# Balanced routing on one core: the leftover search counts with the experts on the partitions and the thresholds in columns, and VectorE takes the digit with a 32x32 turn

## The chip, the cores and the metric

The kernel runs on one core of one Trainium2 chip. The metric is device time in microseconds (us) for one launch. Three runs of the kernel before gave 488.05 us as the median, with 486.91 and 488.65 us as the ends. A profiled execution took 487.56 us; the span between its first and its last instruction is 485.7 us.

## The reference, cut to what matters

Two blocks follow each other. The first is a gated linear attention (4 batches, 8 heads, 768 steps, head width 48). Its output is read as 3072 tokens of width 384. The second is a mixture of 8 experts with a hard balance: every expert takes exactly 384 tokens.

```
logits = x @ w_gate                       # 3072 x 8
order = np.argsort(-logits.flatten())
for idx in order:                         # best pair of token and expert first
    tok, e = idx // E, idx % E
    if assigned[tok] >= 0 or counts[e] >= cap: continue
    assigned[tok] = e; counts[e] += 1
for e in range(E):
    h = np.maximum(x[assigned == e] @ w1[e], 0.0)
    out[assigned == e] = h @ w2[e]
```

The loop over all pairs is serial. The kernel does it in rounds: every token that is still free votes for its best open expert, and a search finds the logit above which all votes can be granted because the fullest expert just reaches 384.

## The kernel before, in words

**Stages.** Attention runs to about 169 us of the span. Then one full search over all 3072 tokens (24 blocks of 128) closes the first expert, and all tokens that this search places get their slots. The tokens that it doesn't place, at most 768 (`NL` = 6 blocks of 128), are the leftovers; their rows of logits are fetched by six indirect DMAs into `lg` (lines 678 to 682). Rounds 1 to 7 of the leftover search (the loop at line 712) assign them, one round per expert that closes. The list of places is completed after that (lines 739 to 755), the rows of the third block of each expert can be fetched, and the remaining matmuls run.

**The expert matmuls as filler.** Two blocks of the experts 0 to 4 are already known before the leftover search, and their work is cut into pieces which wait in a queue, `pe_work`: a piece T turns one block of rows (three transposes, line 484), a piece H is one product of the up projection (line 495; 24 per expert), and a piece O is one product of the down projection (line 506; 16 per expert). One H or O piece is two MATMUL instructions in the trace, since the operands are 32 bit wide. All of this part stands under a manual schedule, so each engine executes its instructions in the order in which the program writes them.

**The planner that sets this order.** Two clocks in us, `pe` and `dve`, run along while the program is written. `V(n, cost)` (line 458) moves `dve` forward by the planned cost of VectorE instructions. `PE(cost)` (line 461) stands ahead of each group of small matmuls that depends on VectorE: it takes pieces from the queue until `pe` reaches `dve` + 0.1, then adds the group's own cost to `pe`, and sets `dve` to at least `pe` + 0.22. A piece costs 0.65 (T), 0.44 (H) or 0.65 (O) by this clock. It is arithmetic on constants; no run changes it.

**One digit of the search before** (`search`, line 550, called at line 718 with `n` = 6). The logits are scaled to whole numbers below 2^20, and the threshold is found in 4 digits of 5 bits. For each digit, VectorE writes `above`, 6 x 31 flags for each partition: is this token at or above threshold 1 to 31. TensorE counts with six matmuls (line 564), the flags as the weights (31 columns) and the one-hot choices of the expert (8 columns) as the moving operand; a seventh (line 567) adds what each expert holds already. The counts stand with thresholds on 31 partitions and experts in 8 columns. VectorE takes the largest over the experts (`most`, line 570) and compares with 384 (`filled`, line 571). A matmul with the constant weights `units[d]` (line 574) sums the flags over the partitions and writes the new `base` to all 128 partitions, from which `above` of the next digit subtracts.

**Around the digits.** After four digits, `sure` (line 720) marks the placed tokens, `more` and `now` (lines 726, 727) count them per expert, one matmul with `ones16` (line 731) sums over the partitions, and `pen`, `held`, `gone` and `lg` (lines 732 to 736) close full experts and placed tokens for the next round. At the head of the next round, `ov` and `ch` (lines 715, 716) are the best open logit of each token and its one-hot expert.

Of the kernel before, what the change touches and what calls it, by code (L numbers as in the profile page):

```python
# [12 lines left out]
FP16 = mybir.dt.float16  # L13
I32 = mybir.dt.int32
ALU = mybir.AluOpType
# [5 lines left out]
GONE = -1.0e9  # L21
# [3 lines left out]
def kernel(  # L25
# [11 lines left out]
    nc = tc.nc  # L37
# [3 lines left out]
    E = moe_w_gate.shape[1]  # L41
# [7 lines left out]
    NT = N // 128  # L49
    CAP = N // E  # L50
# [239 lines left out]
    DIGITS, BITS = 4, 5  # L290
    TH = (1 << BITS) - 1
    RANGE = float(1 << (DIGITS * BITS))
    NL = 6
    NQ = NL + TE * E
    NA = 5
    KC = E + 1

    def tt(out_, a, b, op):
        nc.vector.tensor_tensor(out=out_, in0=a, in1=b, op=op)  # L299

    def ts(out_, a, s1, op0, s2=None, op1=None):
        kw = {} if op1 is None else {"op1": op1}
        nc.vector.tensor_scalar(out=out_, in0=a, scalar1=s1, scalar2=s2, op0=op0, **kw)

    def stt(out_, a, s, b, op0, op1):
        nc.vector.scalar_tensor_tensor(out=out_, in0=a, scalar=s, in1=b, op0=op0, op1=op1)

    def reduce(out_, in_, op):
        nc.vector.tensor_reduce(out=out_, in_=in_, axis=AX_X, op=op)

    def rt(shape, name, dtype=FP32, bufs=2):
        return route.tile([128] + shape, dtype, name=name, tag=name, bufs=bufs)

    def mid_of(t, n):
        return t.unsqueeze(1).to_broadcast((128, n) + tuple(t.shape[1:]))

    def last_of(t, n):
        return t.unsqueeze(len(t.shape)).to_broadcast(tuple(t.shape) + (n,))
# [5 lines left out]
    ones16, after16 = const([128, 128], FP16, "ones16"), const([128, 128], FP16, "after16")  # L324
# [16 lines left out]
    def ramp(n, name, step, base):  # L341
        t = const([128, n], FP32, name)
        ts(t[:], linef[:, 0:n], float(step), ALU.mult, float(base), ALU.add)
        return t

    first = ramp(E, "first", -1, E)
    code_e = ramp(E, "code_e", -TE, NL + TE * (E - 1))
    steps, units = [], []
# [95 lines left out]
    def fast():  # L444
# [4 lines left out]
        def bank(name, tag):  # L449
            return psum.tile([128, 512], FP32, name=name, tag=tag, bufs=BUFS[tag])  # L450
# [7 lines left out]
        def V(n=1, cost=0.21):  # L458
            clock["dve"] += n * cost

        def PE(cost):
            while pe_work and clock["pe"] < clock["dve"] + 0.1:
                piece()
            clock["pe"] = max(clock["pe"], clock["dve"] + 0.1) + cost
            clock["dve"] = max(clock["dve"], clock["pe"] + 0.22)
# [84 lines left out]
        def search(over, choice, n, held):  # L550

            base = bank("base", "b")
            for d in range(DIGITS):
                above = rt([n, TH], f"above{n}", FP16)
                a, s = last_of(over, TH), mid_of(steps[d][:], n)
                if d == 0:
                    tt(above[:], a, s, ALU.is_ge)
                else:
                    stt(above[:], a, base[:, 0:1], s, ALU.subtract, ALU.is_ge)
                V(cost=0.15 + n * TH / 700)  # L560
                r = bank("cnt", "r")
                PE(0.03 * n + 0.1)
                for c in range(n):
                    nc.tensor.matmul(out=r[0:TH, 0:E], lhsT=above[:, c, :], rhs=choice[:, c, :],  # L564
                                     start=(c == 0), stop=(c == n - 1 and held is None))
                if held is not None:
                    nc.tensor.matmul(out=r[0:TH, 0:E], lhsT=ones16[:, 0:TH], rhs=held[:],
                                     start=False, stop=True)
                most, filled = rt([1], "most"), rt([1], "filled", FP16)
                reduce(most[0:TH], r[0:TH, 0:E], ALU.max)  # L570
                ts(filled[0:TH], most[0:TH], CAP - 0.5, ALU.is_ge)
                V(2)
                PE(0.06)
                nc.tensor.matmul(out=base[:, 0:1], lhsT=units[d][0:TH, :], rhs=filled[0:TH],
                                 start=(d == 0), stop=(d == DIGITS - 1), skip_group_check=True)
            return base

        def positions(kind, nk, n, code, notfirst_, held):

            incl = rt([nk, n], f"incl{n}", FP16)  # L580
            P = bank("P", "r")
            w = nk * n
            Pv = P[:, 0:w].rearrange("p (k c) -> p k c", c=n)
            PE(0.1)
            nc.tensor.matmul(out=Pv, lhsT=after16[:], rhs=kind[:], start=True, stop=False)
            nc.vector.tensor_tensor_scan(incl[:].rearrange("p k c -> p (k c)"), notfirst_,
                                         kind[:].rearrange("p k c -> p (k c)"), 0.0,
                                         op0=ALU.mult, op1=ALU.add)
            V(cost=0.1 + w / 350)
            PE(0.2)  # L590
            nc.tensor.matmul(out=Pv, lhsT=ones16[:], rhs=incl[:], start=False, stop=held is None)
            if held is not None:
                nc.tensor.matmul(out=Pv, lhsT=ones16[:], rhs=last_of(held, n), start=False,
                                 stop=True)
            sums = P[:, 256:256 + nk]
            total = rt([nk], f"total{n}", FP16)
            nc.vector.tensor_copy(out=total[:], in_=incl[:, :, n - 1])
            own, pos = rt([nk, n], f"own{n}"), rt([n], f"pos{n}")
            tt(own[:], Pv, kind[:], ALU.mult)
            reduce(pos[:], own[:].rearrange("p k c -> p c k"), ALU.max)  # L600
            q, line, blk = rt([n], f"q{n}"), rt([n], f"line{n}", FP16), rt([n], f"blk{n}", FP16)
            ts(q[:], pos[:], 0.5 - 64.0, ALU.add, 1.0 / 128.0, ALU.mult)
            ts(q[:], q[:], 12582912.0, ALU.add, -12582912.0, ALU.add)
            stt(line[:], q[:], -128.0, pos[:], ALU.mult, ALU.add)
            tt(blk[:], q[:], code, ALU.add)
            V(9)
            return total, line, blk
# [36 lines left out]
        with tc.manual_schedule(engines=engines):  # L644
            idle = rt([3 * 128], "idle", FP16, 1)
            nc.gpsimd.memset(idle[:], 1.0)
            base = search(over0[:], choice0, NT, None)
# [5 lines left out]
            total, line, blk = positions(kind, KC, NT, code[:],  # L653
                                         notfirst[:].rearrange("p k c -> p (k c)"), None)
# [18 lines left out]
            for e in range(1, NA):  # L673
                for i in range(2):
                    p = place_of(e, i)
# [19 lines left out]
            nc.vector.tensor_copy(out=val_l[:], in_=found[:, 0:NL])  # L695
            m = bank("m", "r")
            nc.tensor.matmul(out=m[:, 0:KC], lhsT=ones16[:], rhs=total[:], start=True, stop=True)
            few = rt([E], "few", FP32, 1)
            nc.vector.memset(few[:], 0.0)
            ts(few[:, 0:NA], m[:, 1:1 + NA], 2 * 128 - 0.5, ALU.is_lt)  # L700
# [4 lines left out]
            ts(pen[:], m[:, 1:KC], CAP - 0.5, ALU.is_ge, GONE, ALU.mult)  # L705
            held, got = rt([E], "held", FP16), rt([NL, E], "got", FP32, 1)
            stt(held[:], pen[:], 0.0, total[:, 1:KC], ALU.is_ge, ALU.mult)
            nc.vector.memset(got[:], 0.0)
            clock["dve"] = 15.0
            ts(lg[:], lg[:], low_scale[:, 0:1], ALU.add, low_scale[:, 1:2], ALU.mult)  # L710
            tt(lg[:], lg[:], last_of(gone[:], E), ALU.add)
            for rnd in range(1, E):
                tt(lg[:], lg[:], mid_of(pen[:], NL), ALU.add)
                ov, ch = rt([NL], "ov"), rt([NL, E], "ch", FP16)
                reduce(ov[:], lg[:], ALU.max)
                tt(ch[:], lg[:], last_of(ov[:], E), ALU.is_equal)
                V(3, 0.23)
                base = search(ov[:], ch, NL, held)
                sure, gone = rt([NL, E], "sure"), rt([NL], "gone")
                stt(sure[:], last_of(ov[:], E), base[:, 0:1], ch[:], ALU.is_ge, ALU.mult)  # L720
                tt(got[:], got[:], sure[:], ALU.add)
                V(2)
                if rnd == E - 1:
                    break
                more, now = rt([E], "more"), rt([E], "now", FP16)
                reduce(more[:], sure[:].rearrange("p c e -> p e c"), ALU.add)
                tt(now[:], held[:], more[:], ALU.add)
                V(2)
                PE(0.05)
                m2 = bank("m2", "r")  # L730
                nc.tensor.matmul(out=m2[:, 0:E], lhsT=ones16[:], rhs=now[:], start=True, stop=True)
                ts(gone[:], ov[:], base[:, 0:1], ALU.is_ge, GONE, ALU.mult)
                pen, held = rt([E], "pen"), rt([E], "held", FP16)
                ts(pen[:], m2[:, 0:E], CAP - 0.5, ALU.is_ge, GONE, ALU.mult)
                stt(held[:], pen[:], 0.0, now[:], ALU.is_ge, ALU.mult)
                tt(lg[:], lg[:], last_of(gone[:], E), ALU.add)
                V(4)

# [17 lines left out]
            for e in range(E):  # L756
                for i in range(2 if e < NA else 0, TE):
# [6 lines left out]
                             stop=False)  # L764
# [613 lines left out]
```

## Time and profile before

| what | value |
|---|---|
| median of three runs | 488.05 us (486.91 to 488.65) |
| the profiled execution's own time | 487.56 us |
| its span | 485.7 us |
| TensorE (PE) busy, share of the span | 454.8 us, 94% |
| VectorE (DVE) busy | 157.2 us, 32% |
| leftover search, first count to last base | 205.9 to 302.3 us of the span |
| mean granted clock of TensorE | 0.971 |

Times in the profile are us from the start of the span. PE is TensorE's matmuls, PEld its weight loads, DVE VectorE, ACT ScalarE, POOL GpSimd. In a row of the timeline stand the start, the length, the engine, the line of the kernel, the operation, what is written and read with sizes, how many instructions of this kind were merged, and in brackets how long the engine stood idle just before and what ended that. Lengths of matmuls include a tail that overlaps the next one, so the distance between starts says what one costs.

### The profile page before, as it was taken

Reading aid. Unit: us, or ns where it says so; the run is one execution under the profiler, and the core shown is the slowest. Engines: PE = TensorE matmul, PEld = TensorE weight load, DVE = VectorE, ACT = ScalarE, POOL = GpSimd, SP = SyncE. Lnnn points to the kernel's source line nnn. Section 1 sums busy time; section 2 is a strip of 40 time slices with the busy share of each in tenths; the row PEclk is TensorE's granted clock in tenths of the full one; section 3 lists DMA queues with packets and bytes.
Section 4 is the critical chain, followed back from the end, with each engine's and each line's share of the span. In section 5 each row is a group of like instructions: output and inputs, shape, how many; then the busy total and the mean of one; then the engine's idle time right before and its main releaser. Section 6 shows DMA issues by size and latency. Waiting matters only on the chain.

```text
span 485.7 us, 11676 instructions
## 1 busy us (share of the span) xinstructions
PE 454.8 (94%) x4996; PEld 323.1 (67%) x4996; DVE 157.2 (32%) x507; ACT 138.1 (28%) x366; POOL 105.2 (22%) x157
## 2 busy tenths in 40 slices
PE   2999999999999859999999999899999999999991
PEld 1778888887888635857566665768877656556550
DVE  7466655665667754123233332300000000000000
ACT  3455554555433100212121211213322312212200
POOL 3134333343223004710000101320003301301010
PEclk9999999999999857999999999999999999999996
DMA  9997999799931187960000000215993200200000
GB/s 152 188 166 164 190 198 202 158 194 263 245 141 52 55 305 267 312 225 17 18 17 1 32 1 16 68 51 198 301 319 95 66 0 34 66 16 34 0 34 20
DMA packets 118541, 59.28 MB, mean 122 GB/s; under 512 B 101840, under 2 KB 113104, under 8 KB 118480
## 3 DMA queue, kind: packets, MB, share of 16 engines
q1 hardware_dynamic: 111760, 44.06, 37.2%
q0 software_dynamic: 3264, 9.56, 6.5%
q10 hardware_dynamic: 3456, 4.82, 2.8%
q8 instruction: 41, 0.67, 0.6%
q14 instruction: 20, 0.16, 0.1%
HBM read 48.89 MB, written 9.54 MB: 120 GB/s over the span
## 4 chain that ended last, share of the span: by engine, by line
PE 73%; issue 15%; POOL 4%; DVE 4%; DMA 2%; ACT 0%; POOLq 0%; DVEq 0%
PE O L506 20%; PE H L495 19%; PE Y L225 5%; PE T L171 4%; PE A L208 4%; PE L L139 4%; PE L L143 3%; PE Y L235 2%; PE dS L190 2%; PE X L249 2%; PE cnt L564 2%; PE X L260 2%; DMA lg<-xd,at_l 2%; PE Xe L484 1%; POOL out_dram L512 1%
## 5 line engine op out<-in xcount | busy, mean ns | idle before, releaser
L495 PE MATMUL H<-xeT,w 128*128 128x256 f32 (+2 forms) x624 | 135.2, 369 | 2.0 <-DVE beyond L783 1.4
L506 PE MATMUL O<-w,hT 128*128 128x384 f32 x384 | 136.6, 494 | 0.0
L495 PEld LDWEIGHTS H<-xeT,w 128*128 128x128 f32 x624 | 97.7, 191 | 28.9 <-issue 1.6
L506 PEld LDWEIGHTS O<-w,hT 128*128 128x128 f32 x384 | 68.8, 190 | 37.0 <-issue 0.4
L512 POOL DMA_INDIRECT out_dram<-o,tok x24 | 23.5, 978 | 222.6 <-ACT o L511 218.4
L499 ACT ACTIVATE hT<-H 128x256 f32<-128x256 f32 (+2 forms) x104 | 38.2, 367 | 98.2 <-PE H L495 96.9
L213 DVE COPY_PREDICATED am<-mask,A 128x512 f32<-128x512 int32 x48 | 32.5, 732 | 30.8 <-PE A L208 30.8
L511 ACT COPY o<-O 128x384 f32<-128x384 f32 x24 | 11.5, 478 | 80.0 <-PE O L506 78.2
L545 POOL DMA_INDIRECT xe<-xd,tok x24 | 23.1, 963 | 42.6 <-DVE numb L299 29.2
L163 POOL TENSOR_TENSOR kg<-k,ek 128x384 f32<-128x384 f32 x24 | 25.6, 1067 | 26.7 <-ACT ek L151 20.9
L139 PE MATMUL L<-g,wcum 128*128 128x384 f32 x48 | 23.0, 564 | 7.4 <-DVE linef L333 7.4
L225 PE MATMUL Y<-v,am 128*64 128x48 f32 x768 | 27.7, 224 | 0.2 <-issue 0.2
L225 PEld LDWEIGHTS Y<-v,am 128*64 128x64 f32 x768 | 24.5, 138 | 4.2 <-issue 4.0
L208 PE MATMUL A<-qT,kT 48*64 48x128 f32 x768 | 27.1, 278 | 0.1
L487 ACT COPY xeT<-Xe 128x384 f32<-128x384 f32 x24 | 11.4, 478 | 44.0 <-PE Xe L484 44.0
L143 PEld LDWEIGHTS L<-ind,g 128*64 128x64 f32 x384 | 13.9, 144 | 14.1 <-issue 14.1
L208 PEld LDWEIGHTS A<-qT,kT 48*64 48x64 f32 x768 | 21.7, 137 | 0.6 <-issue 0.3
L564 PEld LDWEIGHTS <-above 128*31 128x31 f16 x264 | 8.8, 97 | 19.0 <-issue 10.5
L150 ACT ACTIVATE eq<-dl 128x384 f32<-128x384 f32 x24 | 12.6, 523 | 27.7 <-DVE dl L148 27.2
L148 DVE TENSOR_SCALAR dl<-L 128x384 f32<-128x384 f32 x24 | 13.4, 558 | 20.6 <-PE L L143 20.6
L157 POOL TENSOR_TENSOR gl<-spans 128x4 f32<-128x4 f32 x20 | 4.0, 199 | 66.4 <-DVE logits L265 49.7
L171 PE MATMUL T<-ident,qg 128*128 128x128 f32 x96 | 16.6, 299 | 1.8 <-DVE qg L162 1.8
(179 smaller groups left out, 462.0 us busy)
## 6 DMA issues: line engine op xcount, KB each, us to landing
w<-in_moe_w_dram SPq DMA_DIRECT2D x16, 1536.0 KB, 9.7
xd<-x ACTq DMA_DIRECT2D x24, 196.0 KB, 3.4
f<-in_f_logit_dram SPq DMA_DIRECT2D x24, 192.0 KB, 4.6
q<-in_q_dram SPq DMA_DIRECT2D x24, 192.0 KB, 4.6
k<-in_k_dram SPq DMA_DIRECT2D x24, 192.0 KB, 4.7
v<-in_v_dram SPq DMA_DIRECT2D x24, 192.0 KB, 4.7
xe<-xd,tok POOLq DMA_INDIRECT x24, 3.7
out_dram<-o,tok POOLq DMA_INDIRECT x24, 2.6
```

The source lines that it names most:

```text
L139: nc.tensor.matmul(out=Lv, lhsT=wcum[:], rhs=g[:, :, 0:DH], start=True, stop=True)
L143: nc.tensor.matmul(out=ends[DP * r:DP * r + DP, :, hp], lhsT=g[:, 2 * hp + r, :], rhs=ind[:], start=True, stop=True)
L163: nc.gpsimd.tensor_tensor(out=kg[:, :, 0:DH], in0=G["k"][:], in1=ek[:], op=ALU.mult)
L171: nc.tensor.transpose(out=T[:, 128 * hp:128 * hp + 128], in_=t[:, 2 * hp:2 * hp + 2, :].rearrange("t h d -> t (h d)"), identity=ident[:])
L208: nc.tensor.matmul(out=A[par][HC * j:HC * j + HC, 128 * hp:128 * hp + 128], lhsT=G["kT"][rows, hp, HC * j:HC * j + HC], rhs=G["qT"][rows, ...
L213: nc.vector.copy_predicated(am[:, par], mask[:].unsqueeze(1).to_broadcast((128, HP, 128)), A[par][:].rearrange("s (a t) -> s a t", t=128))
L225: nc.tensor.matmul(out=Y[par][HC * j:HC * j + HC, DH * hp:DH * hp + DH], lhsT=G["am"][:, par, hp, HC * j:HC * j + HC], rhs=G["v"][:, 2 * h ...
L495: nc.tensor.matmul(out=L["H"][:, 0:w], lhsT=slots[e][0][:, d, 128 * ft:128 * ft + 128], rhs=xT[:, d, 0:w], start=(d == 0), stop=(d == DC - 1))
L499: nc.scalar.activation(out=hT[:, ft, 0:w], in_=L["H"][:, 0:w], func=AF.Relu)
L506: nc.tensor.matmul(out=L["O"][:, 0:D], lhsT=hT[:, ft, 128 * i:128 * i + 128], rhs=slots[e][1][:, ft, :], start=(ft == 0), stop=(ft == FC - 1))
L512: nc.gpsimd.indirect_dma_start(out=outs[next(tiles)][:, :], out_offset=bass.IndirectOffsetOnAxis(ap=token(e, first_block + i), axis=0), in ...
L545: nc.gpsimd.indirect_dma_start(out=t[:], out_offset=None, in_=xd[:, :], in_offset=bass.IndirectOffsetOnAxis(ap=token(e, i), axis=0))
```

## The change

Counts of the leftover search are turned around. The weights are now the choices, with each token's 8 flags of the expert repeated 16 times to 128 columns (`choices`, made once per round by VectorE's `copies_of`), and the moving operand is `above`, 32 columns of thresholds. The count of an expert so stands on 16 partitions at once, with its thresholds in 32 columns. What an expert holds is added as a value per partition (`there`), which one more matmul per round makes from the repeated totals. VectorE compares (`full`), sums over the thresholds (`most`, which is this expert's digit), turns 32x32 blocks (`turned`) so that every partition sees all experts, and takes the largest (`digit`). The next digit works on a scaled rest `z` instead of `base`. The seventh round has no search: all that is left is placed. The general first search and all else stay as they are. The kernel is otherwise the same file; line numbers behind the edits move.

```diff
+    TR = 32
+    parts_of = ramp(TR, "parts_of", 1.0 / TR, 1.0 / TR)
...
+        def copies_of(t, name):
+            shape = list(t.shape[1:])
+            c = rt(shape[:-1] + [128 // E, E], name, FP16, 1)
+            nc.vector.tensor_copy(out=c[:], in_=t.unsqueeze(len(shape)).to_broadcast(
+                (128,) + tuple(shape[:-1]) + (128 // E, E)))
+            V(cost=0.15 + 128 * (shape[0] if len(shape) > 1 else 1) / 1400)
+            return c
+
+        def placed(sums):
+            there = rt([1], "there")
+            ts(there[:], sums, CAP - 0.75, ALU.min)
+            V()
+            return there
+
+        def search_rest(over, choice, there):
+            z = rt([NL], "z")
+            ts(z[:], over, 32.0 / RANGE, ALU.mult)
+            V()
+            for d in range(DIGITS):
+                above = rt([NL, TR], "above_r", FP16)
+                s = mid_of(parts_of[:], NL)
+                if d == 0:
+                    stt(above[:], last_of(z[:], TR), 1.0 / TR, s, ALU.mult, ALU.is_ge)
+                    choices = copies_of(choice, f"in_line{NT}")
+                else:
+                    stt(above[:], last_of(z[:], TR), digit[:, 0:1], s, ALU.subtract, ALU.is_ge)
+                V(cost=0.15 + NL * TR / 950)
+                r = bank("cnt", "r")
+                PE(0.25)
+                for c in range(NL):
+                    nc.tensor.matmul(out=r[:, 0:TR],
+                                     lhsT=choices[:, c].rearrange("p r e -> p (r e)"),
+                                     rhs=above[:, c, :], start=(c == 0), stop=(c == NL - 1))
+                if d:
+                    nz = rt([NL], "z")
+                    ts(nz[:], z[:], digit[:, 0:1], ALU.subtract, 32.0, ALU.mult)
+                    z = nz
+                full, most = rt([TR], "full_r"), rt([1], "most_r")
+                ts(full[:], r[:, 0:TR], there[:], ALU.add, CAP - 0.5, ALU.is_ge)
+                reduce(most[:], full[:], ALU.add)
+                turned, digit = rt([TR], "turned"), rt([1], "digit")
+                nc.vector.transpose(out=turned[:], in_=most[:].to_broadcast((128, TR)))
+                reduce(digit[:], turned[:], ALU.max)
+                V(4)
+            return z, digit
...
+            totals = copies_of(total[:, 1:KC], "sums_r")
+            nc.tensor.matmul(out=m[:, KC:KC + 1], lhsT=totals[:].rearrange("p r e -> p (r e)"),
+                             rhs=ones16[:, 0:1], start=True, stop=True)
...
+            there = placed(m[:, KC:KC + 1])
...
-                base = search(ov[:], ch, NL, held)
                 sure, gone = rt([NL, E], "sure"), rt([NL], "gone")
-                stt(sure[:], last_of(ov[:], E), base[:, 0:1], ch[:], ALU.is_ge, ALU.mult)
+                if rnd == E - 1:
+                    stt(sure[:], last_of(ov[:], E), 0.5 * GONE, ch[:], ALU.is_ge, ALU.mult)
+                    tt(got[:], got[:], sure[:], ALU.add)
+                    V(2)
+                    break
+                z, digit = search_rest(ov[:], ch[:], there)
+                stt(sure[:], last_of(z[:], E), digit[:, 0:1], ch[:], ALU.is_ge, ALU.mult)
                 tt(got[:], got[:], sure[:], ALU.add)
                 V(2)
-                if rnd == E - 1:
-                    break
...
-                PE(0.05)
+                nows = copies_of(now[:], "sums_r")
+                PE(0.08)
                 m2 = bank("m2", "r")
                 nc.tensor.matmul(out=m2[:, 0:E], lhsT=ones16[:], rhs=now[:], start=True, stop=True)
-                ts(gone[:], ov[:], base[:, 0:1], ALU.is_ge, GONE, ALU.mult)
+                nc.tensor.matmul(out=m2[:, E:E + 1], lhsT=nows[:].rearrange("p r e -> p (r e)"),
+                                 rhs=ones16[:, 0:1], start=True, stop=True)
+                ts(gone[:], z[:], digit[:, 0:1], ALU.is_ge, GONE, ALU.mult)
...
+                there = placed(m2[:, E:E + 1])
```

## The prediction, made before the changed kernel ran

> **What bounds the kernel now.** I read the busy times of the page first, then busy time by stretch, the waits inside the leftover search, and last the timeline of single digits.
>
> ```profile
> PE 454.8 (94%) x4996; PEld 323.1 (67%) x4996; DVE 157.2 (32%) x507; ACT 138.1 (28%) x366; POOL 105.2 (22%) x157
> ```
>
> ```profile
> 205.90:302.30 96.40, 96.38 (x526) 59.30 (x526) 30.76 (x149) 16.70 (x40) 7.68 (x8) 1.00 0.12 44
> ...
> 315.00:485.70 170.70, 160.35 (x682) 106.37 (x680) 0.00 (x0) 37.54 (x95) 25.61 (x27) 0.98 0.27 89
> ```
>
> In these rows stand the stretch and its length, then busy time and instructions of PE, PEld, DVE, ACT and POOL, the clock, the DMA share and GB/s. From the first count (205.9) to the last base (302.3) TensorE is busy for 96.38 of 96.40 us at the full clock; VectorE for a third of that. So the search's chain is covered by expert pieces, and what it costs is the TensorE time it takes between them. The waits agree (total us, times, longest):
>
> ```profile
> DVE most L309 <- PE cnt L567: 31.5, 28, 1.5
> ...
> DVE above L306 <- PE base L574: 22.0, 21, 1.3
> ...
> PEld L574 <- issue: 11.4, 28, 0.5
> ```
>
> VectorE waits for TensorE at both ends of each digit. TensorE waits for VectorE hardly at all, but its weight loader stands idle up to 0.5 us ahead of each small matmul of this kind, for no semaphore.
>
> How much of the 96.4 us is search? The same stretch, for lines 495 (H), 506 (O) and 484 (T) alone:
>
> ```profile
> 205.90:302.30 96.40, 38.98 (x146) 25.44 (x146) 1.00 0.12 44
> ```
>
> ```profile
> 205.90:302.30 96.40, 49.44 (x126) 21.23 (x126) 1.00 0.12 44
> ```
>
> ```profile
> 205.90:302.30 96.40, 4.04 (x24) 2.96 (x24) 1.00 0.12 44
> ```
>
> Two instructions make an H or O piece, three a T: 73 H, 63 O, 8 T. Their undisturbed pace, from runs of them in the chain that ended last, and T from two starts in the timeline:
>
> ```profile
> 275.42 2.69 PE H L495 x12
> ...
> 330.94 3.87 PE O L506 x12
> ```
>
> ```profile
> 323.15 0.49 PE L484 MATMUL Xe<-ident,xe 128*128 128x128 f32 x3
> 323.48 0.81 PE L506 MATMUL O<-w,hT 128*128 128x384 f32 x2
> ```
>
> H is 2 x 2.69/12 = 0.448 us, O 2 x 3.87/12 = 0.645, T 0.33. So pieces take 73 x 0.448 + 63 x 0.645 + 8 x 0.33 = 76.0 us, and the search **interrupts** them for 96.4 - 76.0 = **20.4 us**. One digit shows where it goes:
>
> ```profile
> 223.62 0.30 PE L564 MATMUL cnt<-ch,above 128*31 128x8 f16 x6
> ...
> 223.78 0.17 PE L567 MATMUL cnt<-held,ones 128*31 128x8 f16 x1
> ...
> 223.88 1.13 PE L495 MATMUL H<-xeT,w 128*128 128x256 f32 x4
> 223.98 0.15 DVE L309 TENSOR_REDUCE most<-cnt 31x1 f32<-31x8 f32 x1 [0.90 <-PE cnt L567]
> 224.17 0.14 DVE L303 TENSOR_SCALAR filled<-most 31x1 f16<-31x1 f32 x1
> ...
> 224.94 0.17 PE L574 MATMUL base<-filled,unit 31*128 31x1 f16 x1
> ...
> 225.15 0.42 DVE L306 SCALAR_TENSOR_TENSOR above<-ov,base,step 128x186 f16<-128x186 f32 x1 [0.83 <-PE base L574]
> ...
> 226.10 0.30 PE L564 MATMUL cnt<-ch,above 128*31 128x8 f16 x6
> ```
>
> From count to count 2.48 us with four H (1.79): 0.69 lost. Seven counts take 0.26, the base 0.10; the other 0.33 are two gaps of 0.16, between the last piece's end and a matmul whose weights are 31 columns or 31 rows.
>
> **The change, part by part.** All pieces must run in any case, so only interruptions and new stalls move the end; after 315 us TensorE and ACT only consume what is queued.
>
> *Removed:* all 20.4 us, that is 28 counts with 28 bases, and six sums `m2`.
>
> *Added counts:* 24 digits (the seventh round has none) of six matmuls with 128 weight columns in f16 and 32 moving columns, no base. The nearest rows are the last sort's six matmuls with such weights, and other full f16 weights between pieces:
>
> ```profile
> 302.36 1.99 PE L495 MATMUL H<-xeT,w 128*128 128x256 f32 x8
> 304.19 0.19 PE L585 MATMUL P<-kind,after 128*128 128x48 f16 x1
> ...
> 308.75 0.37 PE L631 MATMUL tokens<-numb,in_line 128*128 128x24 f16 x6
> 308.96 1.54 PE L495 MATMUL H<-xeT,w 128*128 128x256 f32 x6
> ```
>
> ```profile
> 217.16 1.56 PE L506 MATMUL O<-w,hT 128*128 128x384 f32 x4
> ...
> 218.55 0.17 PE L731 MATMUL m<-now,ones 128*128 128x8 f16 x1
> ...
> 218.58 0.89 PE L506 MATMUL O<-w,hT 128*128 128x384 f32 x2
> ```
>
> Six matmuls displace 0.21 us (0.035 each). The gap ahead of full weights is 304.19 - 302.36 - 8 x 0.224 = 0.04 behind H (I take 0.05) and 218.55 - 217.16 - 4 x 0.3225 = 0.10 behind O; the f16 sum itself takes 0.03. The planner's arithmetic, run by hand, puts 12 counts behind an H and 12 behind an O or T: 12 x 0.26 + 12 x 0.31 = 6.8 us. The six sums have one matmul more: 6 x (0.10 + 0.07) = 1.0. Together **7.8 us**. Ends: the two-column and thirty-column sorts give other prices; the dearer one is
>
> ```profile
> 186.88 1.52 PE L631 MATMUL tokens<-numb,in_line 128*128 128x30 f16 x24 [0.46 <-DVE numb L299]
> 188.23 4.61 PE L641 MATMUL nothing<-idle,ones 128*128 128x384 f16 x18
> ```
>
> with 1.35/24 = 0.056 each: 24 x (0.34 + 0.10) + 1.3 = 11.8 us. At the low end no gap at all: 24 x 0.21 + 0.5 = 5.5 us. I take 0.035, the row at the same place and clock.
>
> The Trainium skill has a rule against this: "TensorE: Matmul & The Clock Gate", section "LDWEIGHTS (loading the stationary operand)", prices a weight load by its columns, 1/1.2 ns each, so 128 columns would be 107 ns where 31 were 26. By that estimate a count is 0.64 us plus its gap, the additions 18.7 us, and the time 486.3 us. The six sort loads above went by at 0.035 each, so the trace speaks against it here; the same page's section on Fast Weight Load excepts full 16-bit loads.
>
> *The chain on VectorE,* which must stay under the pieces. Rows of the groups (last numbers: busy us, mean ns, idle before):
>
> ```profile
> L306 DVE SCALAR_TENSOR_TENSOR above<-ov,base,step 128x186 f16<-128x186 f32 x21 | 8.8, 418 | 22.0 <-PE base L574 22.0
> ...
> L306 DVE SCALAR_TENSOR_TENSOR sure<-ov,base,ch 128x48 f32<-128x48 f32 x7 | 1.9, 273 | 6.7 <-PE base L574 6.7
> ...
> L309 DVE TENSOR_REDUCE more<-sure 128x8 f32<-128x48 f32 x6 | 1.4, 230 | 0.0
> ...
> L299 DVE TENSOR_TENSOR in_line<-line,pairs 128x768 f16<-128x768 f16 x1 | 0.6, 551 | 0.0
> ...
> L303 DVE TENSOR_SCALAR found<-tokens 128x30 f32<-128x30 f32 x1 | 0.2, 190 | 1.6 <-PE tokens L631 1.6
> ...
> L309 DVE TENSOR_REDUCE worst<-bad 128x1 f32<-128x17 f32 x1 | 0.2, 170 | 0.0
> ```
>
> Between two counts stand `full` (0.19, as `found`), `most` and `digit` (0.17 each, as `worst`), the turn, and `above` (0.43 for 192 elements). No row shows a turn; it reads and writes 32 elements, so I take 0.20, with 0.17 and 0.55 (768 elements) as ends. The skill's "VectorE: DVE Perf Modes", section "The three transpose paths", has 311 ns for 128 x 128 in bf16; by it the sum is the same, since the cover below takes 0.11 more. `full` starts 0.20 behind the last count (223.78 to 223.98), so 0.40 behind the first; five operations are 1.16, four gaps of 0.04 (223.98 + 0.15 to 224.17) 0.16, and I put 0.1 for the way back: the next count can start 1.82 us after this one. `nz` fits while TensorE counts. The planner has meanwhile moved `dve` by 0.22 + 0.84 + 0.35 + 0.1 = 1.51, which takes four H or three pieces with O: TensorE returns after 0.21 + 1.79 + 0.05 = 2.05 (9 such digits), 0.21 + 1.94 + 0.10 = 2.25 (6), or with a T 1.93 (3). **Cover** 0.23, 0.42, 0.11: no stall. Ahead of `m2` come `sure`, `got`, `more`, `now` and the copy `nows` instead of `above`, in all about 2.5 us; six groups of four to six pieces last 2.26 to 3.2, so one stall of 0.24. Ahead of a round's first count stand `there` (0.19), `z` (0.2) and `choices` (0.55 as `in_line`; 0.35 to 0.95 if twice as fast or slow per element) more than before, under 3.5 to 3.9 us of pieces: covered. Only in round 1 does TensorE already wait:
>
> ```profile
> 205.92 0.31 PE L564 MATMUL cnt<-ch,above 128*31 128x8 f16 x6 [0.47 <-DVE above L299]
> ```
>
> There one more O piece (0.65) stands against `z`, `above` + 0.1 and `choices`, 0.85: 0.2 more. `totals` and `there` ahead of the first H, and `parts_of` at the start, lie where VectorE idles. If the cover is gone, each of them costs its length.
>
> **Sum:** 487.56 - 20.4 + 7.8 + 0.24 + 0.2 = 475.4. The profiled execution lies 0.49 us under the median of the runs, within their spread; I forecast **475.5 us**. Its own range by the ends: 472.6 to 479.9.
>
> **Rivals.**
> *A, the chain pokes out a little.* If turn and reductions cost 0.5 us more per digit, H digits stall 0.27, O 0.08, T 0.39, and the `m2` groups 1.6 in all: 9 x 0.27 + 6 x 0.08 + 3 x 0.39 + 1.6 = 5.7, less the 0.24 counted, so 480.9. For it: thin cover; against it: every short row is under 0.28.
> *B, weight loads cost by the column.* Six unhidden loads per count, from the 0.64 above: 486.3. Against it stand 308.75 to 308.96.
> *C, slower: VectorE's chain sets the pace.* The cover of 24 digits and sums is 6.5 us in all; with x more per digit the stall is 24x - 6.5, and it eats the gain of 12.1 from x = 0.78. At x = 1.2, a turn of 1.4 us, over twice the longest row above (0.55), the time is 475.4 + 22 = 497.5. Nothing near this size in the rows does so.
> *D, the gain is given back later,* by rows or weights that come no earlier: 487.6. Against it: those loads are set off by TensorE's own progress, and after 315 us it runs on at 94%, the rest being the last output's way.
> *E, it doesn't do what it says:* another threshold trips the guard `beyond`, and the general path makes it far longer.
>
> **Chances.** Forecast 0.68, A 0.14, B 0.05, C 0.05, D 0.06, E 0.02. Less than 0.3% (1.5 us) can't be told from no change: B is on that edge. Faster 0.86, same 0.07, slower 0.07. The range takes in the ends and most of A: 472.5 to 481.
>
> **What would show it.** Right: from first count to last sum TensorE is still fully busy; no row of line 574's kind; distance from count to count about 2.05 us with four H and 2.25 with three O; no idle time ahead of weight loads; the last count of the search some 23 us earlier while more pieces are left behind it. Wrong: waits of the counts for `above`, a turn over 0.4 us, six counts displacing over 0.4 us, or TensorE idle after the search.

## The result, and the profile after

The changed kernel takes 473.0 us (median of four runs, 471.59 to 475.17); the kernel before took 487.81 us in the same comparison. The ratio is 0.9701, with a 95% interval of 0.9657 to 0.9745, so the change is faster by 14.8 us. The forecast was 475.5 us with a range of 472.5 to 481.0. The profiled execution took 471.59 us, with a span of 469.7 us.

Busy time by stretch of the changed kernel, columns as in the prediction: first the general search and the lists up to the first leftover count, then the leftover search to its last sum, then the part behind the guard's flag (the number that the kernel reads to learn whether it needs its general path).

```profile
169.15:205.33 36.18, 28.28 (x249) 20.56 (x250) 14.27 (x53) 4.10 (x11) 15.20 (x16) 0.81 0.88 289
205.33:276.66 71.33, 71.26 (x415) 51.63 (x416) 46.19 (x218) 14.93 (x36) 6.38 (x8) 1.00 0.15 55
...
289.62:469.70 180.08, 169.72 (x724) 114.60 (x724) 0.00 (x0) 39.87 (x101) 28.37 (x30) 0.98 0.26 87
```

TensorE is still busy without a break in the search, though VectorE now works 46.2 of 71.3 us there (30.8 of 96.4 before). The order of the program puts 72 H, 49 O and 6 T pieces into this stretch: 72 x 0.448 + 49 x 0.645 + 6 x 0.33 = 65.86 us. The **interruptions** are 71.33 - 65.86 = **5.5 us**, where the kernel before had 20.3.

One digit with H pieces, and two starts of counts with O pieces, from the timeline:

```profile
218.11 0.30 PE L611 MATMUL cnt<-above_r,in_line 128*128 128x32 f16 x6
...
218.26 1.97 PE L497 MATMUL H<-xeT,w 128*128 128x256 f32 x8
218.45 0.25 DVE L303 TENSOR_SCALAR full_r<-cnt,there 128x32 f32<-128x32 f32 x1 [1.89 <-PE cnt L611]
218.74 0.19 DVE L309 TENSOR_REDUCE most_r<-full_r 128x1 f32<-128x32 f32 x1
218.96 0.21 DVE L622 STREAM_TRANSPOSE turned<-most_r 128x32 f32<-128x32 f32 x1
219.20 0.19 DVE L309 TENSOR_REDUCE digit<-turned 128x1 f32<-128x32 f32 x1
...
219.42 0.42 DVE L306 SCALAR_TENSOR_TENSOR above_r<-z,digit,parts_of 128x192 f16<-128x192 f32 x1
...
220.07 0.30 PE L611 MATMUL cnt<-above_r,in_line 128*128 128x32 f16 x6
```

```profile
207.51 0.30 PE L611 MATMUL cnt<-above_r,in_line 128*128 128x32 f16 x6
207.67 2.18 PE L508 MATMUL O<-w,hT 128*128 128x384 f32 x6
...
208.83 0.42 DVE L306 SCALAR_TENSOR_TENSOR above_r<-z,digit,parts_of 128x192 f16<-128x192 f32 x1
...
209.69 0.30 PE L611 MATMUL cnt<-above_r,in_line 128*128 128x32 f16 x6
```

From count to count 1.96 us with four H (1.79), 2.18 with three O (1.94). Six counts displace 0.15 us; the gap ahead of them is 0.02 behind H and 0.08 behind O. VectorE's `above_r` is done at 219.84, 0.23 us before TensorE starts the next count; with O pieces the same chain leaves 0.44 (209.25 to 209.69), and with a T 0.12. Where VectorE is late, as in the runs with more turns below, the count follows 0.05 us behind `above_r`, so of these 0.18, 0.39 and 0.07 are to spare. The cover is thin, and it holds.

The waits in this part (the last number is the longest):

```profile
DVE full_r L303 <- PE cnt L611: 18.2, 24, 2.1
...
PEld L611 <- issue: 2.0, 9, 0.2
...
PE H L497 <- DVE beyond L843: 1.6, 1, 1.6
...
PE cnt L611 <- DVE in_line L583: 1.1, 1, 1.1
```

VectorE waits for TensorE in each of the 24 digits, and no row has a count that waits for `above_r`: TensorE never waits for the chain between two digits. The idle time of the weight loader ahead of this search's groups is down from 11.4 us for the bases alone to 2.0 us. TensorE has two larger waits left: for the copied choices of the first round, and for the guard's flag, which it had before.

The two profiled executions differ by 15.97 us. The interruptions make 20.3 - 5.5 = 14.8 of it; the first H piece starts 1.84 us earlier (192.34 against 194.18), a difference ahead of all that the change touches but `totals` and `parts_of`; the first wait takes 0.6 back (1.07 for 0.47) and the flag 0.2. Of the 1.84 us, 1.29 stand already at the first count of the general search (169.15 against 170.44), and no run shows where they come from.

### The profile page after: what moved, and what is told of

The parts are those of the page before. It is cut to its first block, busy times and chain, and to the rows that moved or that the text cites. A ratio compares the mean times of both kernels' runs of the same rounds, so it can differ in the third digit from the quotient of the medians.

```text
span 469.7 us, 11611 instructions
## 1 busy us (share of the span) xinstructions
PE 436.0 (93%) x4923; PEld 319.1 (68%) x4923; DVE 174.7 (37%) x588; ACT 138.2 (29%) x366; POOL 105.6 (22%) x157
## 4 chain that ended last, share of the span: by engine, by line
PE 72%; issue 15%; DVE 5%; POOL 4%; DMA 2%; ACT 0%; POOLq 0%; DVEq 0%
PE O L508 20%; PE H L497 19%; PE Y L225 5%; PE T L171 5%; PE A L208 4%; PE L L139 4%; PE L L143 3%; PE Y L235 3%; PE dS L190 2%; PE X L249 2%; PE X L260 2%; DMA lg<-xd,at_l 2%; POOL out_dram L514 1%; PE Xe L486 1%; POOL lg L728 1%
## 5 line engine op out<-in xcount | busy, mean ns | idle before, releaser
L508 PE MATMUL O<-w,hT 128*128 128x384 f32 x384 | 133.1, 490 | 0.0
L497 PE MATMUL H<-xeT,w 128*128 128x256 f32 (+2 forms) x624 | 130.6, 366 | 2.1 <-DVE beyond L843 1.6
L497 PEld LDWEIGHTS H<-xeT,w 128*128 128x128 f32 x624 | 99.2, 191 | 29.0 <-issue 1.6
L514 POOL DMA_INDIRECT out_dram<-o,tok x24 | 23.5, 980 | 214.0 <-ACT o L513 209.8
L143 PEld LDWEIGHTS L<-ind,g 128*64 128x64 f32 x384 | 13.5, 141 | 13.9 <-issue 13.9
L241 ACT COPY x<-Y 128x192 f32<-128x192 f32 x48 | 13.1, 321 | 16.4 <-PE Y L235 15.9
```

The costliest lines, as they stand in the source:

```text
L143: nc.tensor.matmul(out=ends[DP * r:DP * r + DP, :, hp], lhsT=g[:, 2 * hp + r, :], rhs=ind[:], start=True, stop=True)
L497: nc.tensor.matmul(out=L["H"][:, 0:w], lhsT=slots[e][0][:, d, 128 * ft:128 * ft + 128], rhs=xT[:, d, 0:w], start=(d == 0), stop=(d == DC - 1))
L508: nc.tensor.matmul(out=L["O"][:, 0:D], lhsT=hT[:, ft, 128 * i:128 * i + 128], rhs=slots[e][1][:, ft, :], start=(ft == 0), stop=(ft == FC - 1))
L514: nc.gpsimd.indirect_dma_start(out=outs[next(tiles)][:, :], out_offset=bass.IndirectOffsetOnAxis(ap=token(e, first_block + i), axis=0), in ...
```

## The experiments

The later runs are slower as a whole: the kernel before took 497.5 to 499.8 us there, and the changed one 484.3. The difference lies ahead of the search: the changed kernel has 46.95 us from the first general count to the first leftover count where it had 36.18, with a lower granted clock (0.71 against 0.81). Why that is so, no run shows.

```profile
169.15:216.10 46.95, 33.53 (x249) 24.28 (x250) 14.07 (x53) 4.11 (x11) 15.45 (x16) 0.71 0.82 279
216.10:287.42 71.32, 71.25 (x417) 51.61 (x416) 46.19 (x218) 14.93 (x36) 6.15 (x7) 1.00 0.05 18
```

The search itself repeats to 0.01 us (71.32, second row). So each experiment is read twice, by its ratio to the kernel before beside it, and by the length of this stretch.

| run | ratio to before, 95% | search, us | pieces, us | interruptions and stalls, us |
|---|---|---|---|---|
| before | 1 | 96.33 | 76.0 | 20.3 |
| no seventh search | 0.9927 (0.9895 to 0.9959) | 82.62 | 65.2 | 17.4 |
| full weights | 0.9798 (0.9752 to 0.9844) | 85.69 | 76.0 | 9.7 |
| both of these | 0.9787 (0.9728 to 0.9845) | 73.43 | 65.2 | 8.2 |
| the change, again | 0.9690 (0.9651 to 0.9729) | 71.32 | 65.9 | 5.5 |
| counts twice | 0.9743 (0.9705 to 0.9781) | 74.92 | 65.9 | 9.1 |
| one narrow matmul more | 0.9827 (0.9753 to 0.9901) | 76.43 | 65.9 | 10.6 |
| one full matmul more | 0.9722 (0.9684 to 0.9760) | 71.92 | 65.9 | 6.1 |
| two more turns | 0.9808 (0.9742 to 0.9875) | 77.63 | 65.9 | 11.8 |
| four more turns | 1.0040 (1.0006 to 1.0075) | 89.40 | 65.9 | 23.5 |
| two waits filled | 0.9659 (0.9616 to 0.9702) | 71.34 | 65.9 | 5.5 |

Stretches of the kernels without a seventh search end at the sixth round's sum, the two others at the last base. The pieces are worked out from the order of each program (72 H, 48 O and 6 T where it says 65.2).

**The seventh search alone.**

```diff
+                if rnd == E - 1:
+                    stt(sure[:], last_of(ov[:], E), 0.5 * GONE, ch[:], ALU.is_ge, ALU.mult)
+                    tt(got[:], got[:], sure[:], ALU.add)
+                    V(2)
+                    break
                 base = search(ov[:], ch, NL, held)
```

> The kernel before, with the seventh search left out as the change does it; all else old. Theory (each digit interrupts the expert pieces for about 0.70 us, and interruptions are all that the leftover search costs): four digits fewer, -2.8 us, 485.0 us, and the interruption of the remaining 24 digits stays at 0.69 (H) and 0.76 (O). Rival (the digits run for nothing under other work, and the gain came from the shorter chain of one trip per digit): no change, 487.8 us.

Measured 493.53 us beside 497.54: 3.6 us less by the ratio (2.0 to 5.2). The interruptions fall by 2.9 us to 17.4, which is 24 digits of 0.70 and six sums. The digits that remain look as before (the first six rounds take 82.63 us in both traces), here from one count to the next:

```profile
235.09 0.31 PE L564 MATMUL cnt<-ch,above 128*31 128x8 f16 x6
...
237.58 0.31 PE L564 MATMUL cnt<-ch,above 128*31 128x8 f16 x6
```

2.49 us with four H, 0.70 lost. A digit costs its interruption, and the rival of digits that run for nothing falls.

**Full weights in the old search.** The flags stand in 31 columns of a zeroed tile of 128, and all matmuls of the leftover search use 128 columns and rows.

```diff
+    wide = [const([128, NL, 128], FP16, f"wide{i}") for i in range(1)]
...
-                above = rt([n, TH], f"above{n}", FP16)
+                    above, rows_ = wide[0], 128
+                    weights, flags = above, above[:, :, 0:TH]
...
-                    nc.tensor.matmul(out=r[0:TH, 0:E], lhsT=above[:, c, :], rhs=choice[:, c, :],
+                    nc.tensor.matmul(out=r[0:rows_, 0:E], lhsT=weights[:, c, :], rhs=choice[:, c, :],
...
-                nc.tensor.matmul(out=base[:, 0:1], lhsT=units[d][0:TH, :], rhs=filled[0:TH],
+                nc.tensor.matmul(out=base[:, 0:1], lhsT=units[d][0:rows_, :], rhs=filled[0:rows_],
```

> The kernel before, with its two trips per digit and all seven searches, but every small matmul of the leftover search with 128 weight columns and rows: the flags stand in a tile whose other columns are zero, and the sums run over 128 rows. Theory (the gap of 0.16 us ahead of each of these matmul groups belongs to weights of 31 columns or rows, and full weights go by at 0.025 us each as in the changed kernel): per digit about 0.30 instead of 0.70 us, 28 x 0.40 = -11.2 us, 476.6 us, with weight loads no longer idle ahead of the groups. Rival 1 (a gap comes with every group, whatever its weights): no change, 487.8. Rival 2 (weight loads cost by the column): seven loads of 128 columns at 0.108 us, +0.5 us per digit, 502 us.

Measured 487.56 us beside 497.54, 10.0 us less (7.8 to 12.3), and 10.6 us fewer interruptions. The algorithm is untouched: two trips, 31 thresholds, seven rounds. One digit of it:

```profile
229.85 0.29 PE L572 MATMUL cnt<-ch,wide 128*128 128x8 f16 x6
230.01 0.17 PE L575 MATMUL cnt<-held,ones 128*128 128x8 f16 x1
230.03 1.11 PE L498 MATMUL H<-xeT,w 128*128 128x256 f32 x4
230.98 0.17 PE L582 MATMUL base<-filled,unit 128*128 128x1 f16 x1
231.01 1.11 PE L498 MATMUL H<-xeT,w 128*128 128x256 f32 x4
231.95 0.29 PE L572 MATMUL cnt<-ch,wide 128*128 128x8 f16 x6
```

Count to count is 2.10 us, not 2.48. Seven full matmuls take 0.18 where seven narrow ones took 0.26; the base takes 0.03 where it took 0.10; each gap is 0.05 where it was 0.16. The counts were narrow by their columns (31) and the base by its rows (31), and both gaps shrink. Both rivals fall, and with them the price by columns.

**Both edits.**

> The kernel before with both edits: full weights and no seventh search; still thresholds on the partitions, a largest over experts, and the base by a matmul, two trips per digit. If width and the seventh search are the main terms: 24 x 0.30 + 0.6 = 7.8 us of interruptions instead of 20.4, -12.6 us, 475.2 us, so that the turned counts and VectorE's digit add only about 2 us on top in the changed kernel. If the single trip per digit carries the gain: near 485, as with the seventh search left out alone.

Measured 485.00 us, 10.6 us less by the ratio (7.7 to 13.5), which can't be told from the full weights alone by time. The stretch tells them apart: 8.2 us of interruptions, close to the expected 7.8. From here to the changed kernel's 5.5 are 2.7 us, all that the turned counts and VectorE's digit add. By the ratios this last step is 4.8 us, but the two come from different comparisons and their intervals touch. So, taken in this order, of 14.8 us the seventh search is 2.9, the width of the weights 9.2, and the single trip 2.7; with the width first it is 10.6 for the width and 1.5 for the seventh search. The single trip was only priced behind full weights. With narrow ones the base and its gap displaced 0.10 + 0.16 us per digit, so halving the trips there would have been worth some 6 us in 24 digits, an estimate that wasn't run.

**The price of the counts.**

```diff
-                for c in range(NL):
-                    nc.tensor.matmul(out=r[:, 0:TR],
+                for _ in range(2):
+                    for c in range(NL):
+                        nc.tensor.matmul(out=r[:, 0:TR],
```

> The changed kernel with the six counting matmuls of each digit issued twice (the second set overwrites the first). This prices six matmuls with full weights. From the changed kernel's timeline (0.15 us from the first count to the next piece): 24 x 0.15 = +3.6 us, 476.6 us. From the price in the prediction (0.035 us each): 24 x 0.21 = +5.0 us, 478.0 us.

Measured 486.41 us, ratio 0.9743; the stretch is 3.6 us longer, which is 24 x 0.15. Twelve counts to the next piece:

```profile
234.04 0.46 PE L612 MATMUL cnt<-above_r,in_line 128*128 128x32 f16 x12
234.35 1.97 PE L497 MATMUL H<-xeT,w 128*128 128x256 f32 x8
```

A count with full weights and 32 moving columns costs 0.025 to 0.026 us, not the 0.035 of the prediction.

**One matmul more per digit, narrow or full.** It stands ahead of the counts, and its result is not used.

```diff
+                nc.tensor.matmul(out=r[0:31, 64:72], lhsT=ones16[:, 0:31], rhs=ones16[:, 0:8],
+                                 start=True, stop=True)
```

and, for the control, `out=r[:, 64:72], lhsT=ones16[:]`.

> The changed kernel with one more matmul ahead of each digit's counts, with weights of 31 columns and 8 moving columns; its result is not used. Theory (narrow weights bring the gap of 0.16 us where full ones have 0.02 to 0.08): 24 x (0.03 + 0.11) = +3.4 us, 476.4 us, and the weight loader idle ahead of it. Rival (only the number of matmuls and groups counts): 24 x 0.03 = +0.7 us, 473.7 us, the same as with full weights.

> The control of the run with the narrow matmul: the same extra matmul with 128 weight columns. Both theories: 24 x 0.025 = +0.6 us, 473.6 us.

The full one lengthens the search by 0.60 us, as expected. The narrow one lengthens it by 5.1 us, 0.21 per digit and more than the 0.14 expected:

```profile
232.62 0.09 PEld L610 LDWEIGHTS <-ones 128*31 128x31 f16 x1 [0.33 <-issue]
232.62 0.18 PE L610 MATMUL cnt<-ones 128*31 128x8 f16 x1
232.72 0.22 PEld L613 LDWEIGHTS <-in_line 128*128 128x128 f16 x6
232.73 0.32 PE L613 MATMUL cnt<-above_r,in_line 128*128 128x32 f16 x6
...
234.80 0.18 PE L610 MATMUL cnt<-ones 128*31 128x8 f16 x1
```

The gap is paid on both sides. The narrow load waits 0.33 us, ahead of it the piece runs out, and the first full load behind it comes only 0.10 later, where a full neighbour follows after 0.025. Narrow matmuls in a row don't pay it: six counts with 31 columns took 0.16 us before (223.62 to 223.78). The Trainium skill, "TensorEngine Tiling (Array Packing)", section "Key Properties", says that a change of the array's tiling mode drains TensorE. A gap on both sides fits that, but no run here shows that these matmuls change the mode, so the reason for the gap stays open. What the runs do give is its size: 0.2 us per visit of a narrow matmul between full ones.

**The cover of VectorE's chain.** Three or five turns give what one gives.

```diff
+                for i in range(2):
+                    turned_, turned = turned, rt([TR], f"turned{i % 2}")
+                    nc.vector.transpose(out=turned[:], in_=turned_[:])
```

> The changed kernel with the 32x32 turn done three times in a row instead of once in each digit; three turns give what one gives. Each adds about 0.25 us to VectorE's chain, x = 0.5 per digit. Theory (the chain is covered by pieces with 0.23 us to spare in H digits, 0.42 in O digits and 0.11 with a T): stalls as in rival A, +5.5 us, 478.5 us, with waits of the counts for the flags above. Rival (cover is larger, since the planner's pieces leave a spare): +0 to 1 us. Rival (no cover at all): 24 x 0.5 = +12 us, 485 us.

> The changed kernel with five turns in a row per digit instead of one, x = 1.0 us on VectorE's chain. Theory (cover of 24 digits and sums is 6.5 us in all): 24 x 1.0 - 6.5 = +17.5 us, 490.5 us, which is slower than the kernel before: the mechanism of rival C. Rival (other pieces flow into the gap): less than +6 us.

The search grows by 6.3 us with two more turns (5.5 expected) and by 18.1 us with four (17.5 expected); the ratios give 5.9 and 17.5 us over the changed kernel. A turn more costs VectorE 0.246 us, so two and four add 11.8 and 23.6 us to its chain in 24 digits; in both runs 5.5 us of that don't show: this is the cover in all. With four, the kernel is slower than the one before by 0.4% (0.06 to 0.75%), a small difference that is clear of zero: rival C, made to happen. TensorE's waits with two, then with four:

```profile
PE cnt L611 <- DVE above_r L306: 2.2, 12, 0.3
...
PE m L791 <- DVE now L299: 0.4, 1, 0.4
```

```profile
PE cnt L611 <- DVE above_r L306: 10.7, 18, 0.8
...
PE m L791 <- DVE now L299: 2.3, 5, 0.9
```

These waits are less than the growth, since a matmul's row includes a tail that the profile models, and the idle time is counted from its end; the distance between counts is the safer reading.

**The two waits that were left.**

```diff
-            clock["dve"] = 15.0
+            clock["dve"] = 16.3
...
+            for _ in range(4):
+                piece()
             flag = nc.values_load(beyond[0:1, 0:1], min_val=0, max_val=3072)
```

> The changed kernel once more, for its time beside the next ones on the same chip: 473.0 us, ratio to before 0.970.

> The changed kernel with TensorE's two remaining waits in this part filled with pieces: the planner's start clock for VectorE at 16.3 instead of 15.0 (about two more O pieces ahead of the first count), and four pieces ahead of the read of the guard's flag. Theory (TensorE bounds this part, so every wait is a loss): 1.07 us wait ahead of the first count and 1.55 us ahead of the flag go, -2.6 us, 470.4 us. Rival (the later start of the search or of the flag is paid behind): no change.

Measured 482.62 us beside 484.31 for the change and 499.82 for the kernel before, ratio 0.9659: 1.7 us less than the change by the medians, but the intervals overlap, so that by time it stays open. In the trace the flag's wait of 1.5 us is gone: TensorE goes on 0.14 us after the guard's last matmul.

```profile
300.81 0.28 PE L836 MATMUL ends<-span,onesf 128*128 128x1 f32 x2
300.95 5.43 PE L497 MATMUL H<-xeT,w 128*128 128x256 f32 x24
```

The other half of the expectation can't be judged. In these later runs TensorE got its first pieces late, the leftovers' logits were there before it, and the changed kernel had no wait ahead of the first count to begin with.

## Why the prediction was right, point by point

**What bounds the kernel:** right. The search costs what it takes from TensorE, and all of the 20.3 us was interruptions; no run contradicts it, and the changed search repeats to 0.01 us while the part ahead of it moves by 10.8.

**The added counts:** right in kind, too dear. The sum took 0.21 us for six counts and gaps of 0.05 and 0.10; the trace has 0.15, 0.02 and 0.08, and doubling the counts confirms 0.15. With these values 12 x 0.17 + 12 x 0.23 = 4.8 us, plus six sums, makes the 5.5 that were measured, stall included; the sum had 7.8 and 0.24. This term is what was mis-sized. In the profiled execution it makes 2.5 of the 3.8 us between the sum (475.4) and the time (471.59); the earlier first H piece makes 1.84 more, which the prediction couldn't know, and two longer waits give 0.6 back (0.4 over the forecast at the first, 0.2 at the flag). That the median came nearer to the forecast, 473.0 to 475.5, is the spread of the runs: the profiled one was the fastest of four. The row chosen for the price, the last sort's six matmuls, was one sample. It takes 0.22 us in the changed kernel too (284.12 to 284.34), so the sort's matmuls differ from the counts: their weights are every second element of `in_line`, and their moving columns stand apart in `numb`, where the counts' operands lie side by side. Whether that is the cause wasn't tried.

```profile
284.12 0.38 PE L680 MATMUL tokens<-numb,in_line 128*128 128x24 f16 x6
284.34 1.54 PE L508 MATMUL O<-w,hT 128*128 128x384 f32 x4
```

**The gaps:** right. The prediction called the 0.16 us a property of weights with 31 columns or rows, and priced full weights without it; full weights in the old algorithm take 10 us off by themselves (10.0 by time, 10.6 by the stretch). The prediction didn't see that this could be had without turning the counts.

**The chain on VectorE:** right within 0.06 us per row. The turn was put at 0.20 and takes 0.21, `most` and `digit` 0.17 and 0.19, `full` 0.19 and 0.25, `above` 0.43 and 0.42. The errors nearly cancel: from one count to the next possible one the sum had 1.82, and the trace has 1.79 (1.74 to the end of `above_r`, and 0.05 back). The cover was given as 0.23, 0.42 and 0.11 (H, O, T), and is 0.18, 0.39 and 0.07, since the dear counts also made TensorE's return look later: 2.05 and 2.25 us from count to count were forecast, 1.96 and 2.18 were measured. In all it was put at 6.5 us, and is 5.5.

**The first wait:** mis-sized, 0.2 against 0.6 us in the profiled execution, and absent in the later ones. It hangs on when the logits arrive, and not on the change alone: VectorE's first work on them starts 1.10 us earlier than before (203.22 against 204.32), but TensorE's pieces start 1.84 earlier. `choices` took 0.35, not 0.55, so the row of a two-input operation was the wrong neighbour. The stall ahead of the first round's second sum is there (0.2, at 214.09 to 214.32).

```profile
214.09 0.17 PE L788 MATMUL m<-now,ones 128*128 128x8 f16 x1
...
214.32 0.18 PE L789 MATMUL m<-ones,sums_r 128*128 128x1 f16 x1
```

**The rivals:** A didn't come, but is what two more turns make of the kernel. B is refuted by the doubled counts and the full weights. C was put at x = 0.78 us more per digit; with the measured gain and cover it is (14.8 + 5.5) / 24 = 0.85, and four more turns (0.98) crossed over. D didn't come: from the guard's flag to the end it takes 180.05 us where it took 171.85, and the 19 more H pieces that are left for this part account for it (19 x 0.448 = 8.5). E didn't come.

**The signs:** TensorE is busy throughout the search, no row of line 574's kind is left in it, and the last count comes 26.7 us earlier (274.03 against 300.72; some 23 were forecast). Not as forecast, the weight loader still idles 2.0 us ahead of the counts, in 9 places. Of the signs of being wrong, none came: the turn takes 0.21 us and six counts displace 0.15.

## What to carry to other kernels

Where one engine is always busy, price a small step by what it displaces there, from start to start in the timeline, and not by its rows' lengths or by its trips; here the width of a weight tile was worth 9 to 11 us, and the single trip behind it 2.7. Padding small matmuls to full weights is worth a try before an algorithm is turned around. A chain that moves to another engine needs its cover counted per step, since a longer chain cost nothing up to that point here, and its full length beyond it.

## What the runs showed of the hardware that was not expected

- A matmul with 31 weight columns costs 0.2 us between matmuls with full ones, against 0.025 for the same matmul with 128 columns: the gap is paid ahead of it and in part behind it. Among its like it costs 0.027 (six in 0.16 us).
- Full f16 weights of 128 columns with 8 to 32 moving columns go by at 0.025 us each, load included, where the operands lie side by side; six with weights from every second element took 0.22 us (0.036 each).
- A copy of 768 f16 elements per partition, from a source that repeats 8 values 16 times, took 0.35 us, against 0.55 for a two-input comparison of the same size:

```profile
L583 DVE COPY in_line<-ch 128x768 f16<-128x768 f16 x6 | 2.1, 353 | 0.0
```
